# Sixteen weight loads of a fused attention and two-layer kernel, issued by GpSimd instead of SyncE

## The chip, the cores and the metric

The kernel runs on one core of one Trainium2 chip. The metric is the device time of one execution in microseconds. Three runs of the kernel before gave 1612.74, 1613.89 and 1616.48 us; their median is 1613.89 us. Engines are called as in the profile: PE is TensorE (PEld its weight loads), DVE is VectorE, ACT is ScalarE, POOL is GpSimd, SP is SyncE. SPq and POOLq are their instruction queues.

## The reference

An attention without a softmax over pairs of positions (q is normalized per row, k per column, then q times kTv), and two dense layers behind it:

```
q_s = exp(q - max(q, -1)); q_s = q_s / (sum(q_s, -1) + 1e-9)
k_s = exp(k - max(k, 2));  k_s = k_s / (sum(k_s, 2) + 1e-9)
kv  = einsum('bhsd,bhse->bhde', k_s, v)            # 8 x 8 x 64 x 64
x   = einsum('bhsd,bhde->bhse', q_s, kv)           # as 4608 tokens x 512
h   = x @ w_in;  x = relu(h)**2 @ w_out            # first layer, d_ff 2048
h   = x @ w_in2; out = elu(h) @ w_out2             # second layer, d_ff 2048
```

All of it is in float32; q, k and v have 8 batches, 8 heads, 576 positions and 64 features.

## The kernel before

Each float32 operand of a large product is split into a high part (rounded to the matmul's float32r) and a low part (the rest), and a product is three matmuls: high by high, high by low, low by high.

The 4608 tokens are taken in nine blocks of 512. Blocks 0 to 8 each run the first product of layer one, `up`, in sixteen steps j (slots 0 to 15) of twelve matmuls. Block 0 then runs its second product directly, `down`. Blocks 1 to 8 are taken in four pairs (1 and 2, 3 and 4, 5 and 6, 7 and 8): the second product of both is done at once, after `up` of the right block, by seven products of half size instead of eight. The text calls these pair 1 to pair 4. A pair has 56 units, u = 0 to 55, seven products of eight. A unit (`u_mm`, L688) is six matmuls of 512 columns on one weight tile w of 256 KB (high and low parts of 128 x 256), which is streamed from DRAM.

The tensors w1s hold the seven combinations of `w_out` for this. They are made by the kernel itself while blocks 1 and 2 run: DVE makes the sums, ACT the high parts, DVE the low parts, and POOL stores them (`s_hi` L211, `s_lo` L223; the quarters that need no sum are stored by SP, L228). In blocks 3 to 6 the same functions make and store w2s for the second layer, and in blocks 6 to 8 `w_hi` and `w_lo` (L147, L157) store wo1d. All these pass through a ring of four buffers with the tag "st".

The order of work is written out by hand: every engine gets its instructions in the order of the Python calls, and waits at each for the semaphores that it needs. So a wait on an engine's queue holds all that the program puts behind it on that engine. A list of extras is run after each slot j: loads of attention inputs and raw weights on SP, memsets of two columns of the v tiles on POOL (L261, L262), and the conversions above.

`u_load` (L661 to L667) issues the load of one tile w. For u = 0 and 1 the tile takes a buffer "at", for u = 2 and 3 one of the "st" ring, from u = 4 on a buffer that held x for `up` of the right block. The loop over a right block's slots calls it at these places: u = 0 and 1 ahead of `up` of slot 10, u = 2 and 3 after the extras of slot 13, u = 4 to 11 after `up` of slot 15. Later ones are called one for each unit done (`unit`, u + 8). The tiles of u = 0 to 3 are the combination 4 of the column groups j = 0 to 3. For pair 1, the one of j = 3 is written to DRAM by the last `s_hi` and `s_lo` in the extras of slot 13, just ahead of the call for u = 2.

SP issues all loads of w before the change; POOL issues the memsets and the stores of converted weights.

Of the kernel before, what the change touches and what calls it, by code (L numbers as in the profile page):

```python
# [16 lines left out]
P = 128  # L17
# [3 lines left out]
def tile_attention_moe_moe2(  # L21
# [18 lines left out]
    nc = tc.nc  # L40
# [29 lines left out]
    w1s = [dram.tile([P, 7, 2, HW], F32, name=f"w1s{j}") for j in range(NG)]  # L70
# [4 lines left out]
    def f32(ap):  # L75
        return ap.bitcast(F32)
# [584 lines left out]
    def u_load(t, u):  # L661
        if u < NU:
            i, j = SEVEN[u // NG][0], u % NG
            tag, bufs = ("at", 2) if u < 2 else ("st", 4) if u < 4 else (("xh", "xl")[u % 2] + str(u % 8 // 2), 1)
            w = pool.tile([P, 2, 2, P], F32R, tag=tag, bufs=bufs, name=f"w1_{t}_{u}")
            nc.sync.dma_start(f32(w), w1s[j][:, i].rearrange("p s (k f) -> p s k f", f=P))
            ops["w", u] = w  # L667

    def u_split(t, u):
# [424 lines left out]
    with tc.manual_schedule():  # L1094
# [88 lines left out]
        def unit(t, u):  # L1183

            u_mm(t, u)
            if u > 3:
                u_load(t, u + 8)

            now = steps.get(u, [])
            run([x for x in now if x[0] is t_sum])  # L1190
            if u:
                u_split(t, u + 2)
            run([x for x in now if x[0] is not t_sum])
            if u % 2:
                run(extras.get((t, "s", u // 2), ()))

        for t in range(NB):
            paired, final = t >= PAIRED, t == NB - 1
            right = paired and (t - PAIRED) % 2 == 1
            for j in range(NFC):  # L1200
                if right and j == NFC - 6:
                    u_load(t - 1, 0)
                    u_load(t - 1, 1)
# [85 lines left out]
```

## Time and profile before

| | |
|---|---|
| Median of three runs | 1613.89 us |
| Profiled execution | 1612.47 us |
| Its span | 1610.7 us |
| Mean granted TensorE clock | 0.999 |
| PE, DVE, ACT, POOL busy | 1576.0, 1051.3, 974.2, 85.4 us |
| Loads of w from w1s | 224, 256 KB each, median 3.5 us from issue to landing |
| DMA queue of SP | 263.25 MB, 53.3% of 16 engines |
| DMA queue of POOL | 31.46 MB, 4.9% of 16 engines |

The page gives, for the slowest core, each engine's busy time, the costliest groups of instructions by line, and the chain of work that ended last. A matmul of 512 columns is shown with 0.39 us, but matmuls are pipelined and start every 0.23 us; a wait of PE is therefore read from the distance between two starts. A DMA on POOL is shown as busy for as long as POOL works on it, on SP as an instruction of the queue; in both cases the data land later.

### The profile page before, as it was taken

How to read it: one execution, taken by the hardware profiler on the slowest of the kernel's cores; microseconds unless marked ns; L12 is line 12 of the kernel's file. 1: busy time of each engine (PE TensorE's matmuls, PEld its weight loads, DVE VectorE, ACT ScalarE, POOL GpSimd, SP SyncE). 2: the span in 40 equal slices, each digit the busy share in tenths (PEclk: the TensorE clock that was granted, in tenths of full speed). 3: DMA queues.
4: the chain of work that ended last, by engine and by line, in shares of the span. 5: the costliest groups of instructions: out<-in, count | busy, mean ns of one | idle time of the engine just before them, and what ended most of it. 6: DMA issues, size and time to landing. Idle time of an engine off the chain costs nothing.

```text
span 1610.7 us, 23045 instructions
## 1 busy us (share of the span) xinstructions
PE 1576.0 (98%) x8086; PEld 1335.8 (83%) x8086; DVE 1051.3 (65%) x1658; ACT 974.2 (60%) x1665; POOL 85.4 (5%) x190
## 2 busy tenths in 40 slices
PE   5989999999999999999999999999999999999999
PEld 4767787878778777888888899998989989898997
DVE  7987687777977787773687555555555555555544
ACT  7996665566655775556456555555555565555644
POOL 0001220012100220011000000000000000000000
PEclk9999999999999999999999999999999999999999
DMA  9856576757875685653687565435535544543541
GB/s 244 258 166 227 179 241 193 235 180 249 269 225 174 233 283 176 198 196 119 190 292 252 188 201 185 138 112 156 165 105 150 170 126 121 186 126 110 171 112 58
DMA packets 170354, 296.18 MB, mean 184 GB/s; under 512 B 16640, under 2 KB 60672, under 8 KB 170240
## 3 DMA queue, kind: packets, MB, share of 16 engines
q1 hardware_dynamic: 160640, 263.25, 53.3%
q0 software_dynamic: 9600, 31.46, 4.9%
q8 instruction: 65, 1.06, 0.3%
q14 instruction: 49, 0.40, 0.1%
HBM read 238.03 MB, written 56.62 MB: 183 GB/s over the span
## 4 chain that ended last, share of the span: by engine, by line
PE 80%; issue 7%; DVE 5%; DMA 2%; ACT 2%; POOL 1%; SPq 0%; POOLq 0%; DVEq 0%; ACTq 0%
PE p L843 22%; PE p L688 18%; PE y L905 8%; PE y L906 8%; PE y L904 8%; PE ph L571 4%; PE ph L573 4%; PE ph L572 4%; PE px L415 1%; PE pt L390 1%; DMA raw_wo<-wo_dram 1%; DMA w<-w1s 0%; POOL w2s L211 0%; DVE ul L676 0%; DVE mt_wi L123 0%
## 5 line engine op out<-in xcount | busy, mean ns | idle before, releaser
L843 PE MATMUL p<-x2h,w 128*128 128x384 f32 x1344 | 359.3, 336 | 0.0
L688 PE MATMUL p<-uh,w 128*128 128x512 f32 x896 | 282.9, 392 | 3.0 <-DMA w<-w1s 3.0
L843 PEld LDWEIGHTS p<-x2h,w 128*128 128x128 f32 x1344 | 245.0, 188 | 4.4 <-ACT h L943 0.2
L571 PE MATMUL ph<-xh,wi0h 128*128 128x512 f32 x576 | 230.0, 399 | 0.2 <-ACT B L580 0.2
L573 PE MATMUL ph<-xh,wi0l 128*128 128x512 f32 x576 | 225.5, 391 | 1.4 <-DVE wi0l L155 1.4
L906 PE MATMUL y<-wo,g2l 128*128 128x512 f32 x576 | 226.0, 392 | 0.0
L905 PE MATMUL y<-wo,g2h 128*128 128x512 f32 x576 | 225.7, 392 | 0.0
L843 PE MATMUL p<-x2l,w 128*128 128x384 f32 x672 | 225.5, 336 | 0.0
L572 PE MATMUL ph<-xl,wi0h 128*128 128x512 f32 x576 | 225.0, 391 | 0.1
L904 PE MATMUL y<-wo,g2h 128*128 128x512 f32 x576 | 224.0, 389 | 0.0
L688 PEld LDWEIGHTS p<-uh,w 128*128 128x128 f32 x896 | 168.2, 188 | 40.1 <-issue 3.5
L945 DVE TENSOR_TENSOR h<-p,p 128x384 f32<-128x384 f32 x144 | 79.6, 553 | 182.9 <-PE p L843 182.8
L675 ACT ACTIVATE uh<-B 128x512 fp32r<-128x512 f32 x192 | 121.1, 632 | 105.4 <-PE p L688 59.1
L935 ACT ACTIVATE p<-p 128x384 f32<-128x384 f32 x144 | 69.9, 486 | 188.1 <-PE p L843 188.1
L688 PE MATMUL p<-ul,w 128*128 128x512 f32 x448 | 175.3, 391 | 0.4 <-DVE ul L676 0.2
L676 DVE TENSOR_TENSOR ul<-B,uh 128x512 fp32r<-128x512 f32 x192 | 131.4, 689 | 64.2 <-ACT uh L675 62.9
L580 ACT ACTIVATE B<-ph 128x512 f32<-128x512 f32 x128 | 76.1, 595 | 111.7 <-PE ph L573 110.6
L571 PEld LDWEIGHTS ph<-xh,wi0h 128*128 128x128 f32 x576 | 109.7, 190 | 27.1 <-issue 4.9
L573 PEld LDWEIGHTS ph<-xh,wi0l 128*128 128x128 f32 x576 | 108.4, 188 | 25.4 <-DVE wi0l L155 2.3
L843 PEld LDWEIGHTS p<-x2l,w 128*128 128x128 f32 x672 | 126.2, 188 | 3.9
L906 PEld LDWEIGHTS y<-wo,g2l 128*128 128x128 f32 x576 | 108.0, 188 | 22.8
L572 PEld LDWEIGHTS ph<-xl,wi0h 128*128 128x128 f32 x576 | 108.6, 188 | 21.9 <-DVE xl L492 0.5
(126 smaller groups left out, 2329.7 us busy)
## 6 DMA issues: line engine op xcount, KB each, us to landing
w<-w2s SPq DMA_DIRECT2D x336, 256.0 KB, 3.1
w<-w1s SPq DMA_DIRECT2D x224, 256.0 KB, 3.5
raw_wo<-wo_dram SPq DMA_DIRECT2D x32, 512.0 KB, 4.3
ks<-k_dram SPq DMA_DIRECT2D x32, 320.0 KB, 5.1
vr<-v_dram SPq DMA_DIRECT2D x32, 320.0 KB, 5.8
kt<-kt_dram SPq DMA_DIRECT2D x32, 288.0 KB, 4.2
q<-q_dram SPq DMA_DIRECT2D x36, 256.0 KB, 4.6
out_dram<-o SPq DMA_DIRECT2D x36, 256.0 KB, 2.5
```

The costliest lines, as they stand in the source:

```text
L571: nc.tensor.matmul(ph, hi[:, c], xh[p], start=(p == 0), stop=False)
L572: nc.tensor.matmul(ph, hi[:, c], xl[p], start=False, stop=False)
L573: nc.tensor.matmul(ph, lo[:, c], xh[p], start=False, stop=(p == NP - 1))
L580: nc.scalar.activation(g, ph, AF.Relu)
L675: nc.scalar.activation(hi, x, AF.Copy)
L676: nc.vector.tensor_tensor(lo, x, f32(hi), op=ALU.subtract)
L688: nc.tensor.matmul(accs[side, m], w[:, s, m], x, start=(new and (j, s) == (0, 0) and x is hi), stop=(j == NG - 1 and s == 1), skip_group_c ...
L843: nc.tensor.matmul(acc, w[:, s, k], x[:, k], start=(begin and (k, s) == (0, 0) and x is hi), stop=((k, s) == (1, 1)), skip_group_check=not ...
L904: nc.tensor.matmul(y2[c], gh[:, cs], hi, start=first, stop=False)
L905: nc.tensor.matmul(y2[c], gh[:, cs], lo, start=False, stop=False)
L906: nc.tensor.matmul(y2[c], gl[:, cs], hi, start=False, stop=last)
L945: nc.vector.tensor_tensor(h, part[add], part["bank", i], op=ALU.add)
```

## The change

The tiles u = 0 to 3 of each of the four pairs are issued from the queue of POOL. They are called at the same places, with the same buffers, sizes and addresses. The loads of u = 4 to 55 stay with SP.

```
             w = pool.tile([P, 2, 2, P], F32R, tag=tag, bufs=bufs, name=f"w1_{t}_{u}")
-            nc.sync.dma_start(f32(w), w1s[j][:, i].rearrange("p s (k f) -> p s k f", f=P))
+            (nc.gpsimd if u < 4 else nc.sync).dma_start(f32(w), w1s[j][:, i].rearrange("p s (k f) -> p s k f", f=P))
             ops["w", u] = w
```

## Rows read from the trace of the kernel before

**Rows 1.** The page: engines' busy time, and a group's busy, mean and idle time.
```profile
PE 1576.0 (98%) x8086; PEld 1335.8 (83%) x8086; DVE 1051.3 (65%) x1658; ACT 974.2 (60%) x1665; POOL 85.4 (5%) x190
...
L688 PE MATMUL p<-uh,w 128*128 128x512 f32 x896 | 282.9, 392 | 3.0 <-DMA w<-w1s 3.0
```
**Rows 2.** Timeline of PE, pair 1: start us, us, instruction, idle before.
```profile
239.43 0.39 PE L688 MATMUL p<-uh,w 128*128 128x512 f32 x1
...
243.28 0.39 PE L688 MATMUL p<-uh,w 128*128 128x512 f32 x1
245.18 0.47 PE L688 MATMUL p<-uh,w 128*128 128x512 f32 x1 [1.51 <-DMA w<-w1s]
```
**Rows 3.** Chain of waits, pair 1: start us, us, what.
```profile
238.06 4.07 DMA w1s<-slwo
...
242.28 2.77 DMA w<-w1s
```
**Rows 4.** Timeline of PE, pair 2.
```profile
421.57 0.39 PE L688 MATMUL p<-uh,w 128*128 128x512 f32 x1
...
424.56 0.40 PE L688 MATMUL p<-uh,w 128*128 128x512 f32 x1
426.47 0.47 PE L688 MATMUL p<-uh,w 128*128 128x512 f32 x1 [1.51 <-DMA w<-w1s]
```
**Rows 5.** Chain of waits, pair 2.
```profile
421.15 0.02 SPq L106
...
421.64 4.69 DMA w<-w1s
```
**Rows 6.** Timeline of POOL, pair 1.
```profile
226.46 0.72 POOL L223 DMA_DIRECT2D w1s<-slwo  x1 [2.29 <-issue]
...
238.06 0.72 POOL L223 DMA_DIRECT2D w1s<-slwo  x1
```
**Rows 7.** Timeline of POOL, pair 2.
```profile
408.68 0.57 POOL L218 DMA_DIRECT2D w2s<-shwi  x1 [2.12 <-DVE shwi L217]
...
422.95 0.72 POOL L223 DMA_DIRECT2D w2s<-slwi  x1 [1.35 <-DVE sumswi L189]
```
**Rows 8.** Timeline of POOL, the last store of pairs 3 and 4.
```profile
603.13 0.54 POOL L157 DMA_DIRECT2D wo1d<-sl_wo  x1 [3.42 <-DVE sl_wo L155]
...
773.81 0.54 POOL L157 DMA_DIRECT2D wo1d<-sl_wo  x1 [1.53 <-DVE sl_wo L155]
```
**Rows 9.** One line's instructions: landing of the store issued at 773.81.
```profile
DMA to landing us min/median/max: 2.4/2.4/2.4
```
**Rows 10.** Timeline of PE, first matmul of pairs 3 and 4.
```profile
607.31 0.39 PE L688 MATMUL p<-uh,w 128*128 128x512 f32 x1
...
780.91 0.39 PE L688 MATMUL p<-uh,w 128*128 128x512 f32 x1
```
**Rows 11.** One tensor's instructions: landing of the store issued at 422.95.
```profile
DMA to landing us min/median/max: 5.9/5.9/5.9
```
**Rows 12.** Stretches: engines' busy us (count), granted clock, DMA share, GB/s.
```profile
245.00:247.00 2.00, 1.82 (x8) 1.57 (x9) 1.89 (x3) 0.12 (x1) 0.00 (x0) 1.00 0.93 312
...
425.00:427.00 2.00, 0.53 (x2) 0.48 (x3) 1.97 (x3) 0.63 (x1) 0.00 (x0) 1.00 1.04 383
```
**Rows 13.** Stretches around the fall of the granted clock.
```profile
102.00:104.00 2.00, 0.24 (x3) 0.18 (x2) 2.00 (x5) 0.68 (x2) 0.00 (x0) 0.81 0.96 241
104.00:106.00 2.00, 2.00 (x6) 1.61 (x7) 0.36 (x1) 2.00 (x4) 0.00 (x0) 0.50 0.34 129
106.00:108.00 2.00, 2.00 (x9) 1.41 (x7) 1.78 (x6) 1.90 (x4) 0.00 (x0) 0.84 0.90 240
```
**Rows 14.** Chain of waits, pair 3.
```profile
614.16 0.61 DVE ul L676
...
614.82 5.27 PE p L688 x22
```
**Rows 15.** One line's instructions, L666 from 414 to 430: landing of ten loads.
```profile
DMA to landing us min/median/max: 4.7/5.9/6.3
```

## The prediction, made before the changed kernel was run

> **What bounds the kernel now.** I read the page first, then the matmul timeline at the start of each paired second product, then the chain of waits there, then what POOL and SP do in order at the same place. TensorE is busy for 1576.0 us of the span, and of the idle time that the page lists before the line of the paired products (L688), 3.0 us ended on a DMA of w from w1s [rows 1]. So a change to these loads can give back little and can take more: what it adds to a wait of TensorE goes into the time nearly whole.
>
> There are four paired products, so 16 tiles move, u0 to u3 of each. The 3.0 us lie in two of the four. In pair 1 the first unit starts at 239.43, and 17 matmuls later, at 243.28, the last of u2 starts: 0.227 us a step, so a unit of six is 1.36 us. The first matmul of u3 comes only at 245.18, 1.90 us after that, a loss of 1.67 [rows 2]. The chain shows why: the last spill to w1s goes out on POOL at 238.06 and lands 4.07 us later, at 242.13; SP, which waited for that landing (u3 reads what the spill writes), issues u3 at 242.28, and it lands 2.77 us later [rows 3]. In pair 2 u0 starts at 421.57, and the first matmul of u2 stands at 426.47 after one at 424.56: 1.91 for a step of 0.23, a loss of 1.68 [rows 4]. There nothing is missing in DRAM: SP stands in front of a load of raw weights until 421.15 and can issue u2 only at 421.64; it lands 4.69 us later [rows 5]. Pairs 3 and 4 lose nothing to these loads.
>
> **The change part by part.** It removes 16 issues from SP's order and puts them into POOL's, at the same places of the program. What counts is what stands ahead of them on POOL, and how soon a DMA that POOL issues lands.
>
> *u0 and u1, eight tiles: 0.* They stand ahead of the stores of slot 10. In pair 1 POOL's last store before that is at 226.46 and takes 0.72, so both are out by about 228.5, 11 us before the first unit [rows 2, 6]. In pair 2 the last is the store at 408.68; with memsets and two issues of 0.54 us (what POOL takes for a store of whole 2 KB rows [rows 8]) they are out by about 410.6, 11 us before 421.57 [rows 4, 7]. With the slowest landing used below, 5.9 us, 5 us of cover are left; pairs 3 and 4 have the same distance of six products. They sit in "at" buffers whose last users ended a block before, so they add no wait, and the stores behind them move by an issue at most. If the cover were gone, each us beyond it would be a us of TensorE.
>
> *u2 and u3 of pairs 3 and 4, four tiles: 0.* They now stand behind POOL's last store of the block, at 603.13 and at 773.81, each 0.54 long [rows 8]. So u2 goes out at about 603.7 and 774.4 and u3 0.6 later; the buffers they take are those of the spills two stores earlier. Nothing else is loading then, because SP's next loads wait for TensorE's last products of the block. A POOL store in such quiet landed in 2.4 us [rows 9], so both tiles are there at 606.7 and 777.4, ahead of 610.0 and 783.6, where u2 is due (607.31 and 780.91 plus two units) [rows 10].
>
> *u3 of pair 1: +1.3 us.* The wait for the spill's landing at 242.13 moves with it, from SP to POOL, so it is issued at the same 242.28. Behind the waiting POOL stand only two short memsets of a v tile that nobody needs yet. But SP no longer waits: u4 to u11, which it sent behind u3, now go out as soon as their slots are free, just before 239.43, and fill the DMA engines when u3 comes. The trace has no load from POOL. The bounds from both sides are POOL's stores: 2.4 us with nothing beside it [rows 9] and 5.9 us in the middle of SP's stream in pair 2 [rows 11]. I take 4.1, the landing of POOL's own store in this very place [rows 3], since the stream is thinner here (312 against 383 GB/s) [rows 12]. Then u3 is there at 246.4 and its first matmul at 246.5 in place of 245.18: +1.3. From the bounds: -0.4 to +3.1. u2 of this pair goes out after the store, at 238.78; with the same 4.1 us it is 0.9 late for its turn at 242.15, but u3 waits longer, so that is inside the 1.3.
>
> *u2 of pair 2: +3.2 us.* This is the largest term. SP's obstacle (421.15) is not in POOL's order, but POOL has its own: two stores of slot 13 stand ahead in the program, and the second waits for DVE and is issued at 422.95, to 423.67 [rows 7]. So u2 goes out at 423.67 in place of 421.64, 2.0 us later, into the queue of that store and beside SP's stream, at a DMA share of 1.04 [rows 12]. The store just ahead of it took 5.9 us to land [rows 11]; the bounds are 2.4 us [rows 9] and, where it must wait for that store to land at 428.85 and needs 2.4 more, 431.25. I take 5.9, the nearest row in time and queue: 429.57, first matmul at about 429.7 in place of 426.47, +3.2. Bounds -0.3 to +4.9. u3, 0.54 later, is there before its turn at 431.
>
> *The clock: +1.3 us.* TensorE would then stand from 424.8 to 429.7. The one place in the middle of this trace where I see the granted clock fall shows the price: after 2 us with 0.24 us of matmuls it was 0.50 over 104 to 106 (the 1.2 GHz level) and 0.84 over 106 to 108, while TensorE was busy throughout: (0.50 + 0.16) x 2 = 1.3 us [rows 13]. The waits of today in pairs 1 and 2 left it at 1.00 [rows 12]; one of 4.9 us probably does; one of 3 us in pair 1 I leave out. Bounds 0 and 2.6, for none and both.
>
> *What SP gains: 0.* u4 to u11 come earlier in pair 1, but none of these was waited for. Nor can the next limiter hide any of the sum: in pair 3, where no load is late, a matmul follows DVE's ul at 614.16 [rows 14]; in pairs 1 and 2 the wait for the load covers that already.
>
> Sum: 1.3 + 3.2 + 1.3 = +5.8 us. The profiled execution took 1612.47 us (span 1610.7), so it would take 1618.3; the median of the runs is 1.4 above it, and 1613.89 + 5.8 = 1619.7 is the forecast.
>
> **The rivals.** *Order alone.* Loads from POOL land as quickly as those of SP did. Then u3 of pair 1 is issued and lands as before (0), and u2 of pair 2 takes 4.69 us from 423.67, +2.0, with a wait of 3.7 us and no fall of the clock: 1615.9. For it: in this stretch SP's own loads are no quicker than POOL's store, so the queue itself may cost nothing. Against it: their median is 5.9 too, and 4.7 the least of ten [rows 15]. The Trainium skill, page "DMA: Bandwidth & Descriptors", section "Issuing engines are not separate DMA queues", says that DMAs of all issuers run on the same 16 engines and interleave, so that another issuer saves only issue time; by that rule this rival holds. The same page's Specifications give about 1 us to the first byte from GpSimd and about 0.6 from Sync; by these figures the sum would be an estimated 2 x 0.4 more, +2.8. No run here shows either yet.
>
> *Not slower.* The place is the DMA queue itself: if SP's stream does not hold up POOL's, the tiles land in the quiet 2.4 us. Then u3 of pair 1 comes 0.4 sooner and u2 of pair 2 0.3 sooner: 1613.2. It decides at a landing of 2.66 us in pair 2 (426.33 less 423.67) and 2.77 in pair 1. For it: the quiet row. Against it: a DMA share of 1.04 where u2 comes.
>
> *The early stream hurts more.* SP's stream of u4 to u11, some 3 us earlier than now, also slows the spill at 238.06 that u3 must wait for. With that store at 5.9 us (+1.8), u3 at 5.9 (+1.8 over the 4.1 taken) and a fall of the clock in this pair as well (+1.3), the sum is 5.8 + 4.9 = 10.7: 1624.6; half of the addition, 1622.2, is likelier than the whole.
>
> **How the numbers follow.** Chances: forecast 0.52 (its own range +3.5 to +7.5; without a fall of the clock it is +4.5), order alone 0.23, not slower 0.10, early stream 0.15. A measurement of this kernel can tell about 0.2%, 3.2 us, from no change. The range runs from the third case to the likelier half of the fourth, 1613.2 to 1622.5. Slower by over 0.2%: most of the forecast, all of the fourth and a little of the second, 0.63. Within: the rest of these and nearly all of the third, 0.33. Faster needs 3.2 us, about all that these loads cost today: 0.04.
>
> **What would show it.** In the profile after: idle time of L688 on a DMA of w near 7 us rather than 3.0, in the same two pairs; POOL's w loads behind its stores at about 242.3 and 423.7; landings from POOL of 4 to 6 us there and near 2.4 in pairs 3 and 4; a short stretch at half the granted clock in pair 2. A landing under 3 us in pair 2, a wait for u0 or u1, a wait in pair 3 or 4, or a wait elsewhere that ends because SP's issues are gone would make the prediction wrong.

## The result, and the profile after

The changed kernel takes 1622.37 us (median of 6 runs, 1619.27 to 1624.57), the kernel before 1614.22 in the same comparison (6 runs, 1612.74 to 1616.48). The ratio is 1.0051, with an interval of 1.0041 to 1.0062: 8.2 us slower, 2.7 us beyond the forecast of 1619.7 and just inside its upper end, 1622.5.

The profiled execution is the shortest of the six, 1619.27 us (span 1617.5), 6.8 above the profiled execution of before. The readings below are of these 6.8; the five executions without a profile are taken up further down. First the page: the engines' busy time and the group of the paired products.

```profile
PE 1579.4 (98%) x8086; PEld 1338.2 (83%) x8086; DVE 1051.6 (65%) x1658; ACT 974.7 (60%) x1665; POOL 94.5 (6%) x206
...
L688 PE MATMUL p<-uh,w 128*128 128x512 f32 x896 | 284.3, 394 | 8.1 <-DMA w<-w1s 8.1
```

POOL has 16 instructions more and is busy 9.1 us longer [rows 1], 0.57 us an issue; nobody waits for that time. What counts is the last column: the idle time of L688 on a load of w went from 3.0 to 8.1 us. Busy time of the group rose by 1.4 us for the same 896 matmuls, which is the clock.

PE's timeline at the start of pair 1 and of pair 2 (start us, us, instruction, in brackets the idle time before it and what ended it):

```profile
242.74 0.39 PE L688 MATMUL p<-uh,w 128*128 128x512 f32 x1
244.20 0.47 PE L688 MATMUL p<-uh,w 128*128 128x512 f32 x1 [1.06 <-DMA w<-w1s]
...
245.43 0.40 PE L688 MATMUL p<-uh,w 128*128 128x512 f32 x1
247.96 0.47 PE L688 MATMUL p<-uh,w 128*128 128x512 f32 x1 [2.14 <-DMA w<-w1s]
...
426.95 0.39 PE L688 MATMUL p<-uh,w 128*128 128x512 f32 x1
432.24 0.77 PE L688 MATMUL p<-uh,w 128*128 128x512 f32 x1 [4.91 <-DMA w<-w1s]
432.81 0.63 PE L688 MATMUL p<-ul,w 128*128 128x512 f32 x1
433.23 1.05 PE L688 MATMUL p<-uh,w 128*128 128x512 f32 x2
```

With 0.23 us for a step, pair 1 now loses 244.20 - 242.74 - 0.23 = 1.23 at u2 and 247.96 - 245.43 - 0.23 = 2.30 at u3: 3.5 us in place of 1.67 [rows 2], +1.9. Pair 2 loses 432.24 - 426.95 - 0.23 = 5.06 in place of 1.68 [rows 4], +3.4. And the matmuls that follow in pair 2 stand 0.57 and 0.42 apart (432.24, 432.81, 433.23), not 0.23: the clock has fallen. The chain of waits shows the loads that end these waits (start, us from issue to landing):

```profile
242.25 5.58 DMA w<-w1s
...
426.05 6.06 DMA w<-w1s
```

POOL's timeline says why they are issued when they are:

```profile
238.93 0.73 POOL L223 DMA_DIRECT2D w1s<-slwo  x1
239.65 0.57 POOL L666 DMA_DIRECT2D w<-w1s  x1
242.25 0.57 POOL L666 DMA_DIRECT2D w<-w1s  x1 [2.02 <-PE p L688]
...
425.33 0.73 POOL L223 DMA_DIRECT2D w2s<-slwi  x1 [1.35 <-DVE sumswi L189]
426.05 1.13 POOL L666 DMA_DIRECT2D w<-w1s  x2
```

In pair 1 u2 goes out right behind the store of the last spill, and u3 3.3 us behind that store, at 242.25. The bracket puts the end of its wait down to PE; the landing of the store issued at 238.93 points at that store:

```profile
DMA to landing us min/median/max: 2.7/2.7/2.7
```

The store is there at 241.6, and POOL issues u3 some 0.6 us later, as in three other profiles (pair 1 alone, SP's stream held, both repairs); what fills these 0.6 us the profile does not show. Before, SP issued u3 at 242.28, 0.15 us after the landing of a store that took 4.07 [rows 3]. So from the issue of the store to the landing of u3 it is 8.9 us in place of 7.0: 2.8 more for the landing of u3, twice as long as before, 0.5 more between the two DMAs, and 1.4 less for the store. That is the +1.9 of pair 1. In pair 2 both stand behind the store that waited for DVE (the row that was at 422.95 before [rows 7]), and u2 goes out at 426.05, only 0.9 us before the last matmul that could run without it. SP, which held back behind u3 of pair 1 before, is let go:

```profile
239.76 3.81 SPq L666 DMA_DIRECT2D w<-w1s  x8
```

These are u4 to u11, all issued between 239.76 and 243.6, and u3 is issued in their midst. The stretches (engines' busy us with counts, granted clock, DMA share, GB/s) show both things at once, full DMA engines and the clock:

```profile
246.00:248.00 2.00, 0.04 (x1) 0.07 (x1) 1.71 (x2) 0.55 (x1) 0.00 (x0) 1.00 1.05 410
...
430.00:432.00 2.00, 0.00 (x0) 0.00 (x0) 1.79 (x3) 0.00 (x0) 0.00 (x0) 0.96 1.03 411
432.00:434.00 2.00, 1.76 (x4) 1.49 (x5) 0.00 (x0) 0.00 (x0) 0.00 (x0) 0.50 1.04 404
434.00:436.00 2.00, 2.00 (x7) 1.55 (x6) 0.10 (x1) 0.63 (x1) 0.00 (x0) 0.69 0.39 146
```

The share where u3 of pair 1 waits is 1.05 at 410 GB/s; before it was 0.93 at 312 [rows 12]. In pair 2 TensorE stood still from 427.3 to 432.2 and came back at the half level: 1.76 x 0.50 + 2 x 0.31 = 1.5 us.

**Where the 6.8 us went.** The first matmuls of the four pairs are at 240.25, 424.30, 613.74 and 787.35, against 239.43, 421.57, 607.31 and 780.91 [rows 2, 4, 10]: later by 0.82, 2.73, 6.43 and 6.44. So 0.8 is there before any moved load is used, and already before any is issued: POOL's store of 226.46 [rows 6] is at 227.22 now. It belongs to the execution, not to the change: in three profiles of kernels that differ from the kernel before only from pair 2 on (pair 2 alone; all on SP, late and early), pair 1 starts at 241.5 to 242.3. Between the first two starts it is 1.9, the loss of pair 1. Between the next two it is 3.7: 3.4 of wait and 1.5 of clock, less 0.4 that u1 waited for DVE's ul before (0.49, now 0.12) and less some 0.7, most of it one idle stretch on k's product (L298, 1.9 us in two pieces before, 1.3 in one after). From the start of pair 3 to that of pair 4 nothing is lost. The last 0.4 come behind that: 830.2 us to the end in place of 829.8, and 830.1 or more in every other profile below.

### The profile page after: what moved, and what is told of

It reads as the page before. It is cut to its first block, busy times and chain, and to the rows that moved or that the text cites. A ratio compares the mean times of both kernels' runs of the same rounds, so it can differ in the third digit from the quotient of the medians.

```text
span 1617.5 us, 23060 instructions
## 1 busy us (share of the span) xinstructions
PE 1579.4 (98%) x8086; PEld 1338.2 (83%) x8086; DVE 1051.6 (65%) x1658; ACT 974.7 (60%) x1665; POOL 94.5 (6%) x206
## 4 chain that ended last, share of the span: by engine, by line
PE 81%; DVE 6%; issue 4%; DMA 2%; ACT 2%; POOL 1%; SPq 1%; POOLq 0%; DVEq 0%; ACTq 0%
PE p L843 22%; PE p L688 18%; PE y L905 8%; PE y L906 8%; PE y L904 8%; PE ph L571 5%; PE ph L573 5%; PE ph L572 5%; PE px L415 1%; DMA w<-w1s 1%; PE pt L390 1%; POOL w2s L211 1%; PE pk L298 0%; DVE mt_wi L123 0%; DVE T L656 0%
## 5 line engine op out<-in xcount | busy, mean ns | idle before, releaser
L688 PE MATMUL p<-uh,w 128*128 128x512 f32 x896 | 284.3, 394 | 8.1 <-DMA w<-w1s 8.1
L688 PEld LDWEIGHTS p<-uh,w 128*128 128x128 f32 x896 | 168.9, 188 | 45.8 <-issue 10.8
L688 PE MATMUL p<-ul,w 128*128 128x512 f32 x448 | 175.8, 392 | 0.2
```

Source lines behind the costliest of these rows:

```text
L688: nc.tensor.matmul(accs[side, m], w[:, s, m], x, start=(new and (j, s) == (0, 0) and x is hi), stop=(j == NG - 1 and s == 1), skip_group_c ...
```

## The experiments

Times are against the kernel before on the same chip (medians 1613.5 to 1613.9); a gain or a loss in us is the ratio's. Five of the edits only change the condition of the one changed line; the others move calls, with or without it. My theory was the prediction's: the place in the order and the traffic beside the late tiles cost the time, and u0 and u1 and pairs 3 and 4 cost none. The rivals were that the issuer itself is the cost, that only the order counts, and that SP's early stream does the harm.

**u0 and u1 alone.**

```
-            (nc.gpsimd if u < 4 else nc.sync).dma_start(f32(w), ...)
+            (nc.gpsimd if u < 2 else nc.sync).dma_start(f32(w), ...)
```

> Only u0 and u1 of each pair (eight tiles) go out on POOL. My theory: the loss of the change lies in u2 and u3 of pairs 1 and 2 alone, so this is within 1 us of the kernel before, and TensorE's idle time on a DMA of w stays at 3.0 us. Rival, a load issued by POOL costs something wherever it stands (POOL held up, its stores later): about half of the measured 8.1 us, +4 us.

1614.05 us, ratio 1.0009 (0.9999 to 1.0019), +1.4 us (-0.2 to +3.1): half of the moved tiles cost nothing that can be told, and less than the rival's 4. The execution with the profile is one of the longer ones (1617.81). Nobody waits for u0 or u1 in it. The idle time of L688 on w is 3.2 us, as expected in sum but not in kind: it is one wait in pair 2 and none in pair 1, with a fall of the clock behind it (0.59 and 0.56 over 430 to 434). SP's own u2 of pair 2, issued in its old place, landed after 6.3 us there; in the profile of before, in that of pair 1 alone and in that with SP's stream held it took 4.6 to 4.7. So the landing of one load, with the same issuer and in the same place, differs by 1.6 us between profiles; whether the tiles moved ahead of it have a part in that is not shown.

**u2 and u3 alone.** The same line with `1 < u < 4`.

> Only u2 and u3 of each pair go out on POOL. My theory: all of the loss, +8 us (+7 to +9), idle time on a DMA of w near 8 us as in the changed kernel. Rival, every load on POOL costs its share: +4 us.

1625.09 us, ratio 1.0067 (1.0054 to 1.0079). All of the loss is here, and L688's idle time is that of the whole change and a little more:

```profile
L688 PE MATMUL p<-uh,w 128*128 128x512 f32 x896 | 284.8, 394 | 8.7 <-DMA w<-w1s 8.7
```

The intervals of this ratio and of the whole change's overlap; whether u0 and u1 on POOL give 2 us back beside the other two is not settled. In this profile (1622.08 us, the shortest of its five executions) the clock stays at 1.00 behind the waits of pair 1, of which the longer is 2.4 us, and falls for longer behind the wait of pair 2, which is 5.3:

```profile
434.00:436.00 2.00, 2.00 (x5) 1.56 (x6) 0.00 (x0) 0.00 (x0) 0.00 (x0) 0.50 1.02 392
436.00:438.00 2.00, 2.00 (x6) 1.60 (x5) 0.58 (x1) 0.63 (x1) 0.00 (x0) 0.50 0.03 10
```

With the stretches beside them that is 2.2 us, in place of 1.5 in the changed kernel's profile.

**Pair 1 alone**, with `u < 4 and t == 1` (t counts blocks: 1 is pair 1, 3 is pair 2).

> u0 to u3 of pair 1 alone go out on POOL. My theory: u3 of pair 1 meets SP's stream of u4 to u11, +1.9 us as the two profiles show it, and up to 1.5 more where the granted clock falls there (in the profile after it did not); +2 to +3.5. Rival, the loss sits in pair 2 alone and the 1.9 is given back later: 0. Order alone: 0 to +0.3.

1617.23 us, ratio 1.0022 (1.0013 to 1.0031): +3.6, more than I gave it. The profile has the waits of u2 and u3 and, unlike the changed kernel's, a fall of the clock behind them:

```profile
248.00:250.00 2.00, 1.24 (x3) 1.08 (x4) 0.23 (x1) 0.00 (x0) 0.00 (x0) 0.59 0.56 213
250.00:252.00 2.00, 2.00 (x6) 1.55 (x6) 0.00 (x0) 0.26 (x1) 0.00 (x0) 0.55 0.03 8
```

1.24 x 0.41 + 2 x 0.45 = 1.4 us. The idle time before u2 and u3 of pair 1 is 0.98 and 2.50 in place of 1.51 [rows 2], 2.0 more; together that is 3.4 of the 3.6.

**Pair 2 alone**, with `u < 4 and t == 3`.

> u0 to u3 of pair 2 alone go out on POOL. My theory: u2 stands behind a store that waits for DVE and then lands behind SP's stream, TensorE waits some 5 us and the granted clock falls: +4.4 us as the two profiles show it, +4 to +6. Order alone: +2.0 and no fall of the clock. If the pairs are independent, this and the run for pair 1 add up to the change's 8.1 us.

1619.66 us, ratio 1.0037 (1.0025 to 1.005): +6.0, with one wait of 4.9 us in pair 2. The two pairs add up to 9.6 where the whole change measures 8.2, within what the intervals allow.

**All on SP, but late in pair 2.** SP issues u2 and u3 of pair 2 behind u4 to u7, about where POOL issues them in the changed kernel.

```
-                        for u in range(4, 12):
+                        for u in (4, 5, 6, 7, 2, 3, 8, 9, 10, 11) if t == 4 else range(4, 12):
...
-                    if right and j == NFC - 3:
+                    if right and t != 4 and j == NFC - 3:
```

> All loads are SP's again; in pair 2 alone u2 and u3 are called after u4 to u7, so that SP issues u2 some 2 us later than before, at about the time at which POOL issued it in the changed kernel, behind four loads of its own. My theory, the late place beside SP's stream costs, not POOL's queue: u2 lands some 6 us after its issue, TensorE waits about 5 us, +4 to +6 us, like the run with pair 2 on POOL (+6.0). Rival, POOL's queue is what is slow: u2 lands in 4.7 us as SP's u2 did before, the wait grows by 2.0, +2 us.

1619.38 us, ratio 1.0029 (1.0018 to 1.004), +4.7. No load is POOL's, and the loss of pair 2 is back. SP's u2 goes out at 426.63, 2.5 us behind the first matmul of the pair (in the changed kernel POOL's is 1.8 behind it), and lands 5.84 us later, where POOL's took 6.06:

```profile
427.24 0.40 PE L688 MATMUL p<-uh,w 128*128 128x512 f32 x1
432.61 0.76 PE L688 MATMUL p<-uh,w 128*128 128x512 f32 x1 [4.96 <-DMA w<-w1s]
```

So the two landings differ by 0.2 us, less than one load differs between profiles (the 1.6 above), and the loss has the size of that with pair 2 on POOL (the intervals overlap): the place makes it, not the issuer. The Trainium skill (page "DMA: Bandwidth & Descriptors", section "Issuing engines are not separate DMA queues") says that the DMAs of all issuers run on the same 16 engines and interleave; these two landings agree with it.

**On POOL, but early in pairs 2 to 4.** The changed kernel, with the calls for u2 and u3 moved ahead of what slot 13 adds (its stores), in the blocks behind pair 1.

```
+                    if right and t > 2 and j == NFC - 3:
+                        u_load(t - 1, 2)
+                        u_load(t - 1, 3)
...
-                    if right and j == NFC - 3:
+                    if right and t == 2 and j == NFC - 3:
```

> The changed kernel (u0 to u3 on POOL in all pairs), but in pairs 2 to 4 u2 and u3 are called ahead of the extras of slot 13, so ahead of the stores that wait for ACT and DVE. My theory, POOL's order makes u2 of pair 2 late: it goes out some 7 us earlier, the wait in pair 2 is gone, and with it today's loss there; what is left is pair 1's +3.6 less up to 1.7: +1.5 to +3.5. Rival, loads from POOL land late wherever they stand: pair 2 still waits and the total stays near +8.

1615.42 us, ratio 1.0008 (1.0 to 1.0017), +1.3, a little under what I expected and far from the rival's 8. POOL now issues the two loads of pair 2 at once behind the store before, and does not meet the stores of slot 13, the first of which waits for ACT until 426.31:

```profile
422.32 1.12 POOL L666 DMA_DIRECT2D w<-w1s  x2
426.31 0.72 POOL L211 DMA_DIRECT2D w2s<-shwi  x1 [2.87 <-ACT shwi L210]
```

TensorE waits for no load in pair 2 any more; what is left are the two waits of pair 1:

```profile
PE p L688 <- DMA w<-w1s: 3.1, 2, 2.0
```

Behind these two the clock falls (0.50 and 0.68 over 250 to 254). From the first matmul of pair 1 to that of pair 2 this profile takes 185.5 us in place of 182.1, +3.4, like pair 1 alone; from there to pair 3 it takes 184.0 in place of 185.7.

**Pair 1 on POOL with SP's stream held.** To take SP's loads from in front of u3 without taking a wait away, all of u0 to u11 of pair 1 go to POOL, where they stand behind u3; the other pairs are on SP as before.

```
-            (nc.gpsimd if u < 4 else nc.sync).dma_start(f32(w), ...)
+            (nc.gpsimd if u < (12 if t == 1 else 0) else nc.sync).dma_start(f32(w), ...)
```

> Only pair 1 is changed: u0 to u11 all go out on POOL, so that u4 to u11 stand behind u3 on POOL's queue and not ahead of it on SP's. My theory, u3 was late because SP's stream was let loose ahead of it: u3 now lands within 3 us or so of its issue, the wait of TensorE for u3 is about that of the kernel before, 0 to +1 us. Rival, a load that POOL issues there is slow in itself: as in the run with pair 1 on POOL, u3 lands after 5.6 us, +3.6 us. Should POOL issue u4 to u11 too slowly (0.57 us each), later units would wait, which the timeline of TensorE would show.

1614.05 us, ratio 1.0003 (0.9994 to 1.0011), against +3.6 for pair 1 with the stream ahead. u3 is the first of the loads that POOL issues here (in the chain of nine issues from 244.12 on), and it lands after 3.0 us where it took 5.58; the wait is shorter than the kernel before's [rows 2]:

```profile
244.12 4.82 POOL L666 DMA_DIRECT2D w<-w1s  x9 [2.54 <-issue]
```

```profile
247.26 0.47 PE L688 MATMUL p<-uh,w 128*128 128x512 f32 x1 [1.25 <-DMA w<-w1s]
```

**Both repairs on POOL.** u0 to u3 of all pairs on POOL, as in the change, with the early calls and with u4 to u11 of pair 1 behind u3 on POOL.

```
+            (nc.gpsimd if u < (12 if t == 1 else 4) else nc.sync).dma_start(f32(w), ...)
```

> u0 to u3 of all pairs stay on POOL, with the two repairs: in pair 1 u4 to u11 follow on POOL too, and in pairs 2 to 4 u2 and u3 are called ahead of the extras of slot 13. My theory, the place and SP's stream made all of the loss: 0 against the kernel before (-1 to +1). Rival, something of POOL's issuing remains: +1.5 or more.

1613.04 us, ratio 0.9992 (0.9983 to 1.0001). The 8.2 us are gone with POOL still issuing all 16 tiles, and eight more; the idle time of L688 on w is 0.6 us. It isn't told from the kernel before.

**All on SP, early in pairs 2 to 4**: the kernel before with the same moved calls.

> All loads are SP's; in pairs 2 to 4 u2 and u3 are called ahead of the extras of slot 13, so ahead of the raw weights' load that SP has to wait for. My theory: the wait of 1.7 us in pair 2 goes, and DVE's low parts are late next, by up to the 0.8 us that pairs 3 and 4 lose there: -0.9 to -1.7 us. Rival, the wait moves to the next load: 0.

1613.46 us, ratio 0.9998 (0.9989 to 1.0007). The wait of pair 2 is gone, and no gain can be told: the interval, -1.8 to +1.1 us, holds both my theory and the rival. From pair 2's first matmul to pair 3's this profile takes 184.2 us, against 185.7 in that of before, but 184.7 and 184.9 in two others where pair 2 is unchanged (SP's stream held, pair 1 alone).

**Both waits of before taken away.** The last, and with SP: the early calls; in pair 1's first product another order of columns, so that the tile whose spill is last is wanted two units later; and one of DVE's sums two units later.

```
+    def col(t, u):
+        return (0, 1, 2, 4, 5, 3, 6, 7)[u] if t == PAIRED and u < NG else u % NG
```

> All loads are SP's. In pairs 2 to 4 u2 and u3 are called ahead of the extras of slot 13, and in pair 1 the first product takes its column groups in the order 0, 1, 2, 4, 5, 3, 6, 7, so that the group written last is not needed until the sixth unit (one sum of DVE, T3 for groups 6 and 7, moves two units later for it). My theory: both waits on w go (1.7 us each today), DVE's low parts take back about half: -1 to -2 us. Rival, DVE takes back all: 0.

1614.06 us, ratio 0.9999 (0.999 to 1.0008). No unit waits for a load in this kernel, and yet no gain can be told (-1.6 to +1.3 us). From pair 1's first matmul to pair 2's its profile takes 182.8 us against 182.1 before, though the wait of 1.7 is gone there. Over the whole span the weight loads of the paired products wait 6.8 us for DVE's ul in place of 3.6. In pair 2 (weight-load engine, us in total, times, longest) it is this, where before there was 0.6 of it:

```profile
PEld p L691 <- DVE ul L679: 2.2, 4, 0.7
```

**DVE's sums later**, in all pairs, on top of that: `("T3", (None, None, None, 4)), ("T1", (6, 8, 10, 12))`.

> As the run before it in this list, and in all pairs DVE's sums at the start are called later, as late as their readers allow (T3's last at unit 4 rather than 2, T1's four at units 6, 8, 10 and 12 rather than 3, 5, 7 and 9), so that the low parts of the first units are not behind them. If DVE's sums are the next limiter, the 0.8 to 1.3 us that each pair loses at units 3 to 5 go too: -3 to -5 us in all. Rival, the sums only make later units wait: no better than the run before it.

1618.99 us, ratio 1.0031 (1.002 to 1.0043). A miss, +5.0 us: DVE's sums, put off, make other units wait for ul, in twelve small pieces in all four pairs. That is 2.1 us more than before (0.2); where the rest of the 5.0 lies is not shown.

```profile
PE p L691 <- DVE ul L679: 2.3, 12, 0.2
```

## Why the prediction was right or wrong

It was right in direction and in cause, and the time lies in its range, but only just: the range was to end at the likelier half of the fourth case, which the prediction itself puts at 1622.2, and the 1622.5 that stands there has no working. The measured 1622.37 lies between the two, so that the range held is luck. Two terms were too small.

*u0 and u1: 0.* Right as far as can be told: nothing waits for them in any profile, and moved alone they cost 1.4 us with an interval that reaches to no change.

*u2 and u3 of pairs 3 and 4: 0.* Right in the sum, wrong in a number. Nothing waits there, but the landings are 3.3 us (issue at 609.46, u2 due at 616.5) and 3.6 us (780.87, due at 790.1), not the store's 2.4. Moved to the tight places, that quiet row was no good lower bound.

*u2 of pair 2: +3.2.* Right: +3.4. The two stores ahead, the wait of the second for DVE, and a landing like that of the store (5.9 taken, 6.06 measured). Pair 2 alone and the early call on POOL show that this place is the larger half of the loss; the late call on SP shows that the place does it, not the queue.

*u3 of pair 1: +1.3.* This step failed by size. I saw that SP would let u4 to u11 go ahead of u3, but took the landing of POOL's store, 4.1 us, "since the stream is thinner here (312 against 383 GB/s)". That was the stream of the kernel before, with u3 at its head. The one after runs at 410 GB/s, the landing is 5.58, and the term is +1.9 in the profile. The run with the stream held shows the same issuer at 3.0 us: the stream, not POOL, made the difference (with all loads on SP this was run in pair 2 only). So the landing was taken 1.5 us too short, and that the term is only 0.6 too small is luck: the prediction let the issue stay where it was, while the store ahead of u3 landed 1.4 us sooner (2.7 in place of 4.07) and POOL lost 0.5 between the two. u2's own lateness is inside u3's wait, as written (u2 alone loses 1.23, u3 another 2.30, together the 3.5 above).

*The clock: +1.3.* The price was right for the profiled execution (1.5 in pair 2); how often it falls due is open. "One of 3 us in pair 1 I leave out": the profiles of pair 1 alone and of the early call on POOL show a fall there, those of the changed kernel and of u2 and u3 alone show none. The five executions of the changed kernel without a profile are all longer than the profiled one, by 2.6 to 5.3 us, with a mean granted clock of 0.995 or 0.996 against its 0.998. With the wait of pair 1 as measured (0.6 more) and a fall behind it (1.4) the forecast would have been about 1621.7. But no trace shows where the clock fell in those five. It can be a longer fall in pair 2 (2.2 us with u2 and u3 alone), and it need not be at a moved load: the profiled execution with both repairs, 1613.33 us, has 0.997 with all its low stretches ahead of pair 1 (0.66 over 48 to 52, 0.66 and 0.50 over 104 to 112).

*What SP gains: 0.* Right. And the next limiter, which I took as unable to hide anything: right for the loss. In the other direction it takes back at least a part of what is removed: with both waits gone the weight loads wait longer for DVE's ul, and no gain can be told.

**The rivals.** *Order alone* was right that the issuer costs next to nothing: 6.06 and 5.84 at the late place, 3.0 and 2.77 at the quiet one, a difference of 0.2, besides the 0.5 that POOL took longer between the store's landing and u3. The 0.4 a load that the prediction worked out from the first-byte figures of the Trainium skill (page "DMA: Bandwidth & Descriptors", section "Specifications") is not seen in the landings. Its price fell: it let u2 of pair 2 land after 4.69, a landing that belongs to an earlier place in the stream. *Not slower* is refuted: it needs landings under 2.66 and 2.77 us, and the two took 6.06 and 5.58. Even so they did not simply queue behind SP's loads: the load that SP issued at 425.46, ahead of POOL's of 426.05, landed after 7.4 us, 0.8 behind it. *The early stream hurts more* was right about u3 and, in some executions, about the clock, and wrong about the store that u3 must wait for: it landed after 2.7 us, where it took 4.07.

Open stays how often the clock falls in which pair when no profile is taken, and why u2 and u3 alone measured 10.8 us against 8.2. Each landing is from one execution.

## What to carry to other kernels

An issue that is moved to another engine's queue changes two orders: it now waits for what stands ahead of it there, and what it held back on the old queue is let go. Here the first cost pair 2 (behind a store that waits for DVE), the second pair 1 (behind eight loads that nobody needed yet), and the issuer itself nothing that the time shows (0.9992 with all 16 tiles on POOL in good places). So look for the late tile's neighbours in both queues, put just-in-time loads ahead of stores that wait and ahead of loads that can, and before removing a wait of this size look at which engine is late next.

## What the runs showed of the hardware

A wait can cost more than its length: after TensorE stood for 4.9 us, the granted clock was 0.50 and 0.69 over the next 4 us, 1.5 us on top. After waits of 2.0 to 2.5 us it fell in two kernels' profiles (0.59 and 0.55; 0.50 and 0.68) and not in two others' (1.00). The landing of a 256 KB load went by its place more than by its queue: 2.8 to 3.0 us at the head of the stream, 5.6 to 6.4 us for the late tiles in its midst, from either issuer, and up to 7.4 for SP's own loads beside them. And a load of SP's that no edit had moved took 4.7 us in one kernel's profile and 6.3 in another's.
